# A planned order of instructions with fillers for TensorE, eight weight remainders moved to TensorE and ScalarE, and later due times for the second MoE

## The chip, the cores and the metric

The kernel runs on one core of one Trainium2 chip. The metric is the device time of one execution in microseconds (us). The engines are TensorE (PE in the profile; its weight loads are PEld), VectorE (DVE), ScalarE (ACT), GpSimd (POOL) and SyncE (SP), which issues all DMAs here. TensorE's clock has two levels, 1.2 and 2.4 GHz; the profile gives the granted share of the full one.

## The reference

```python
# x (4,8,768,32), a (4,8,768), B, C (4,8,768,16)
for each chunk:                       # linear attention with decay
    L = exp(cum_i - cum_j) * causal
    y = ((C B^T) * L) x + (C state) * exp(cum)
    state = exp(sum) * state + sum_j B_j x_j * exp(cum_end - cum_j)
x = y as (3072, 256)                  # tokens x model
xn = x / sqrt(mean(x*x) + 1e-6) * rms_g
x = (silu(xn @ w_gate) * (xn @ w_val)) @ w_out       # 256 -> 1536 -> 256
h = x @ w_in                                         # 256 -> 1024
solu = h * softmax(h)
out = layernorm(solu) * g_ln @ w_out2                # 1024 -> 256
```

## The kernel before

The 3072 tokens are 24 units of 128 tokens, and six blocks of four units. A unit passes through the attention (names `lpe`, `lx`, `ls`, `cb`, `mt`, `y`, `s2`, `sbd`), through the RMS norm (`sq`, `ms`, `ts`, `pw`, `rb`, `xc`, `xn`, `xh`, `xl`), a block of 512 tokens through the first MoE (per slice `f` of 128 of the 1536 columns: `gm` and `vm` of TensorE, `th`, `si`, `mu`, `ah`, `al` of ScalarE and VectorE, then `o0`, `o1`), and each unit again through the second MoE (`h`, `mx`, `ex`, `so`, `va`, `t`, `tc`, `tl`, `f`, `out`). Each product is three fp32r matmuls on operands that are split into a high part and a remainder (`xh`/`xl`, `wg_h`/`wg_l`).

The weights come in 26 pieces of 128 x 512 (0, 3, 6, ... gate, 1, 4, 7, ... value, 2, 5, 8, ... output of the first MoE, 18 to 21 and 22 to 25 the second MoE's). The host passes them as 64-bit words. For each piece VectorE makes the fp32 value in three instructions (`wc`, L116, L119, L122), ScalarE copies out the high part (`wh`, L129), and VectorE or GpSimd subtracts for the remainder (`w`, L133). An unused way (`w_lopair`, `w_locopy`, with `VIA_PE` empty) lets TensorE form the remainder in PSUM with the identity and the negative identity, and ScalarE copy it out. Pieces 0 to 17 are wanted during block 0.

The order is no hand-written list. Each operation is entered with an engine, an assumed duration, a due time and its dependences; `plan()` runs through time, takes for the engine that can begin first the ready operation that is due first, and the program is emitted in that order. Every engine then executes its own instructions strictly in the order of the plan, whatever the real durations are. Due times come from `PRO` (where block 0 is to begin), `FIRST` (length of block 0), `Y0`, `YPOS`, `YSPAN` (the attention units), `WGAP` (late weights), `HLAG` and `TAILGAP` (the second MoE's units). `MARGIN` makes the plan assume that a result comes later than it does. Buffers are rings (`BUFS`); an operation that needs a buffer still in use waits. PSUM tiles `y` and `po1` (odd units of block 0) hold one unit's attention output in columns 0 to 255, its state in 256 to 319, its sum of squares in 320 and the broadcast norm factor in 384 to 511.

```python
        if b + 1 < NB:
            lag = [HLAG[min(q, 1)] for q in (b, b + 1)]
            H = start[b + 1] + lag[0] + k * (start[b + 2] - start[b + 1] + lag[1] - lag[0]) / n
```

Of the kernel before, what the change touches and what calls it, by code (L numbers as in the profile page):

```python
# [11 lines left out]
AF = mybir.ActivationFunctionType  # L12
ALU = mybir.AluOpType
# [24 lines left out]
VALATE = 5.0
EARLY = (-1.0, 1.5, 4.0, 6.0)
NPE = 4  # L40
MARGIN = {"PE": 0.5}
CROW = 30.0
WGAP = 8.0
HLAG = (50.0, 26.0)
TRACE = None
BUFS = {"hc": 1, "t": 1, "y": 1, "pg": 1, "pv": 1, "po0": 1, "po1": 1, "L": 2, "bc": 2, "cd": 2, "xb": 2, "e1": 2,
        "u": AHEAD, "th": 3, "wt": 3, "uth": 1, "utl": 1, "xs": 3, "ah": 2, "al": 2, "sbd": 1, "sq": 1,
# [4 lines left out]
def fused_kernel(ctx, tc, aT, xbt, bcT, wg, wv, wo1, rg, wi2, wo2, gl, consts, out):  # L52
# [333 lines left out]
    def at_xc(u):  # L386
        d = st[u]
        d["xts"] = sp.tile([P, 2, P], F32, name="xts", bufs=BUFS["xts"])
        A.activation(d["xts"], d["y"][:, 0:256].rearrange("p (g i) -> p g i", g=2), AF.Copy)

    def at_xn(u):
        d = st[u]
        for g in range(2):
            V.scalar_tensor_tensor(out=d["xts"][:, g], in0=d["xts"][:, g], scalar=rgt[:, g:g + 1],
                                   in1=d["y"][:, 384:512], op0=ALU.mult, op1=ALU.mult)

    def at_xh(u):
        b, k = unit_blk[u]
# [290 lines left out]
    for u in range(NU):  # L689
# [59 lines left out]
        op(f"ts{u}", "DVE", 0.16, Y, (at_ts, u), after=[f"ms{u}"], use=[f"y{u}"])  # L749
        op(f"pw{u}", "POOL", 0.6, Y, (at_pw, u), after=[f"ts{u}"])  # L750
        op(f"rb{u}", "PE", 0.12, Y, (at_rb, u), after=[f"pw{u}"], use=[f"y{u}"])
        op(f"xc{u}", "ACT", 0.42, Y, (at_xc, u), after=[f"y{u}", f"sq{u}"], new=[("xts", f"xt{u}")], use=[f"y{u}", f"xt{u}"])
        op(f"xn{u}", "DVE", 0.6, Y, (at_xn, u), after=[f"rb{u}", f"xc{u}"], use=[f"y{u}", f"xt{u}"])
        op(f"xh{u}", "ACT", 0.42, Y, (at_xh, u), after=[f"xn{u}"] + ([f"xh{u-1}"] if k else []), new=[("xs", f"xs{b}")] if k == 0 else [],
           use=[f"xt{u}", f"xs{b}"])
        op(f"xl{u}", "DVE", 0.43, Y, (at_xl, u, V), after=[f"xh{u}"], use=[f"xt{u}", f"xs{b}"], lock=True)
# [46 lines left out]
    for u in range(NU):  # L803
        b, k = unit_blk[u]
        n = blk[b][1]
        if b + 1 < NB:
            lag = [HLAG[min(q, 1)] for q in (b, b + 1)]
            H = start[b + 1] + lag[0] + k * (start[b + 2] - start[b + 1] + lag[1] - lag[0]) / n
        else:
            H = start[NB] + 14 + TAILGAP * k  # L810
# [88 lines left out]

    op("sf", "PE", 0.7, 5.5, (c_suf,), new=[("t", "pd")], use=["pd"])  # L900
    op("wd", "ACT", 0.35, 5.5, (c_wdec,), after=["sf"], use=["pd"])
    op("cst", "SP", 0.9, 5, (ld_cst,), kb=128)
    op("glt", "SP", 0.45, 40, (ld_glt,), kb=4)
    for u in range(2):
        ops[f"sbd{u}"]["after"].append("cst")
        ops[f"xn{u}"]["after"].append("cst")

    early = [f"lpe{u}.{g}" for u in range(NPE) for g in range(2)] + ["e1p"] + ["cr0", "cr1"]
    ops["wh22"]["after"] += early + ["sf"]

    def plan():
        users = {}
# [44 lines left out]
                t = max(t, dma_end[-8])  # L957
            return t

        while len(order) < len(ops):  # L960
            best = None
            dve = None
            for e, names in ready.items():
                if e == "POOL":
                    names = names + [nm for nm in ready["DVE"] if "alt" in ops[nm] and nm != dve]
                c = [(est(ops[nm], e, MARGIN.get(e, 0.0) if free[e] > PRO else 0.0), nm) for nm in names]
                c = [x for x in c if x[0] < INF]
                if not c:
# [12 lines left out]
            if e != o["e"]:  # L981
                o = ops[nm] = dict(o, us=o["alt"][0], fn=o["alt"][1])
                ready["DVE"].remove(nm)
            else:
                ready[e].remove(nm)
            order.append((t, nm))
            if e == "SP":
                free[e] = t + o["us"]
                dma_free = max(dma_free, t + 1.3) + o["kb"] / 300.0
                end[nm] = dma_free + 1.0  # L990
                dma_end.append(end[nm])
            else:
# [18 lines left out]
    with tc.manual_schedule():  # L1011
        S.dma_start(la, aT)
        S.dma_start(um, consts[:, 0:3 * P])
        S.dma_start(ident, consts[:, 3 * P:4 * P])
        G.memset(ones, 1.0)
        G.memset(mhalf, -0.5)
        wu = pp.tile([P, 512], F32, name="wu", tag="y")
        for _ in range(WARM):
# [7 lines left out]
        V.tensor_scalar(out=cneg, in0=pc2[:, 0:192], scalar1=-1.0, scalar2=None, op0=ALU.mult)  # L1026
        V.tensor_copy(la16[0][:, 0:n16 * NS].rearrange("p (c n) -> p c n", n=NS),
                      la[:, 0:n16].unsqueeze(2).to_broadcast([P, n16, NS]))
        V.tensor_scalar(out=nid, in0=ident, scalar1=-1.0, scalar2=None, op0=ALU.mult)
        seq = plan()  # L1030
        if TRACE is not None:
            TRACE.append(seq)
        for _, nm in seq:
            fn, *a = ops[nm]["fn"]
            fn(*a)


# [62 lines left out]
```

## Time and profile before

| | us |
|---|---|
| median of three runs | 563.78 (561.93 to 565.23) |
| the profiled execution | 565.08 |
| its span, first to last instruction | 563.4 |
| TensorE busy | 546.5 |
| VectorE busy | 390.9 |
| ScalarE busy | 290.3 |
| GpSimd busy | 84.8 |
| mean granted clock of TensorE | 0.981 of full |

A matmul's end is modelled and reaches past the start of the next, so a busy TensorE isn't one at its peak; the distance from start to start tells its pace. The idle time that a row shows in front of an instruction is put down to the engine or DMA whose result came last.

### The profile page before, as it was taken

Reading aid. Unit: us, or ns where it says so; the run is one execution under the profiler, and the core shown is the slowest. Engines: PE = TensorE matmul, PEld = TensorE weight load, DVE = VectorE, ACT = ScalarE, POOL = GpSimd, SP = SyncE. Lnnn points to the kernel's source line nnn. Section 1 sums busy time; section 2 is a strip of 40 time slices with the busy share of each in tenths; the row PEclk is TensorE's granted clock in tenths of the full one; section 3 lists DMA queues with packets and bytes.
Section 4 is the critical chain, followed back from the end, with each engine's and each line's share of the span. In section 5 each row is a group of like instructions: output and inputs, shape, how many; then the busy total and the mean of one; then the engine's idle time right before and its main releaser. Section 6 shows DMA issues by size and latency. Waiting matters only on the chain.

```text
span 563.4 us, 9443 instructions
## 1 busy us (share of the span) xinstructions
PE 546.5 (97%) x3544; PEld 461.1 (82%) x3544; DVE 390.9 (69%) x789; ACT 290.3 (52%) x654; POOL 84.8 (15%) x118
## 2 busy tenths in 40 slices
PE   9879998899999999999999999999999999999996
PEld 8757886687888888888888888888888888888795
DVE  5788999999876776575684574684674574564763
ACT  6437654666555564463474454554543353343464
POOL 2333323212221010110111100110100000000010
PEclk9579999999999999999999999999999999999999
DMA  7464765542022021121120220220200000000000
GB/s 213 132 212 140 216 203 194 182 145 71 14 72 76 2 80 47 43 72 36 54 76 11 75 70 10 80 70 10 72 2 9 10 1 9 11 1 10 9 20 30
DMA packets 44366, 39.33 MB, mean 70 GB/s; under 512 B 3936, under 2 KB 36896, under 8 KB 44320
## 3 DMA queue, kind: packets, MB, share of 16 engines
q1 hardware_dynamic: 44320, 38.72, 22.5%
q8 instruction: 28, 0.46, 0.4%
q14 instruction: 18, 0.15, 0.1%
HBM read 35.37 MB, written 3.34 MB: 69 GB/s over the span
## 4 chain that ended last, share of the span: by engine, by line
PE 81%; DVE 15%; DMA 2%; issue 1%; ACT 1%; SPq 0%; POOL 0%; DVEq 0%; ACTq 0%; POOLq 0%
PE pv L558 15%; PE pg L558 15%; PE po L600 14%; PE ph L436 12%; PE pf L538 12%; PE pt L514 4%; PE pcb L301 3%; DVE wt L119 2%; PE y L326 2%; DVE wt L122 2%; DVE th L580 2%; PE y L321 1%; DVE al L592 1%; DVE th L576 1%; DVE L L307 1%; DVE wt L116 1%
## 5 line engine op out<-in xcount | busy, mean ns | idle before, releaser
L586 ACT ACTIVATE ah<-th 128x512 fp32r<-128x512 f32 x72 | 45.2, 628 | 52.2 <-PE po L600 38.8
L580 DVE TENSOR_TENSOR th<-pv,th 128x512 f32<-128x512 f32 x72 | 49.8, 691 | 29.2 <-PE pv L558 24.1
L592 DVE TENSOR_TENSOR al<-th,ah 128x512 fp32r<-128x512 f32 x70 | 49.3, 704 | 26.0 <-ACT ah L586 25.6
L576 DVE SCALAR_TENSOR_TENSOR th<-th,pg 128x512 f32<-128x512 f32 x72 | 49.1, 682 | 20.0 <-ACT th L572 19.7
L558 PE MATMUL pg<-xh,wg_h 128*128 128x512 f32 x144 | 59.5, 413 | 2.3 <-ACT xh L401 1.2
L600 PE MATMUL po<-ah,wo_h 128*128 128x512 f32 x144 | 60.3, 419 | 0.0
L600 PE MATMUL po<-al,wo_h 128*128 128x512 f32 x144 | 56.7, 394 | 2.3 <-DVE al L592 2.3
L558 PE MATMUL pv<-xh,wv_h 128*128 128x512 f32 x144 | 58.4, 406 | 0.0
L558 PE MATMUL pg<-xh,wg_l 128*128 128x512 f32 x144 | 57.0, 396 | 0.0
L558 PE MATMUL pg<-xl,wg_h 128*128 128x512 f32 x144 | 56.8, 394 | 0.0
L600 PE MATMUL po<-ah,wo_l 128*128 128x512 f32 x144 | 56.7, 394 | 0.0
L558 PE MATMUL pv<-xl,wv_h 128*128 128x512 f32 x144 | 56.5, 392 | 0.0
L558 PE MATMUL pv<-xh,wv_l 128*128 128x512 f32 x144 | 56.4, 392 | 0.0
L572 ACT ACTIVATE th<-pg 128x512 f32<-128x512 f32 x72 | 42.6, 592 | 26.6 <-PE pg L558 26.4
L502 POOL TENSOR_TENSOR sc<-sc,mhalf 128x1 f32<-128x1 f32 x24 | 14.1, 587 | 263.6 <-DVE sc L497 263.6
L237 ACT ACTIVATE L<-L,cneg 128x128 f32<-128x128 f32 x160 | 50.5, 390 | 0.6 <-DMA L<-crow 0.6
L460 ACT ACTIVATE ut<-ph,sc 128x1024 f32<-128x1024 f32 x20 | 22.3, 1116 | 54.5 <-DVE sc L447 54.5
L538 PE MATMUL pf<-wo_h,uth 128*128 128x256 f32 x176 | 49.6, 282 | 0.3 <-DVE utl L528 0.2
L538 PE MATMUL pf<-wo_h,utl 128*128 128x256 f32 x176 | 49.6, 282 | 0.0
L538 PE MATMUL pf<-wo_l,uth 128*128 128x256 f32 x176 | 49.5, 281 | 0.0
L447 DVE TENSOR_REDUCE sc<-ph 128x1 f32<-128x1024 f32 x20 | 24.5, 1225 | 31.7 <-PE ph L436 31.7
L523 ACT ACTIVATE uth<-pt 128x512 fp32r<-128x512 f32 x44 | 26.0, 595 | 31.1 <-PE pt L514 30.9
(138 smaller groups left out, 1225.2 us busy)
## 6 DMA issues: line engine op xcount, KB each, us to landing
L<-crow SPq DMA_DIRECT2D x20, 512.0 KB
stage<-in_wo_dram SPq DMA_DIRECT2D x10, 512.0 KB
xb<-in_xbt_dram SPq DMA_DIRECT2D x24, 192.0 KB
stage<-in_wg_dram SPq DMA_DIRECT2D x6, 512.0 KB
bc<-in_bcT_dram SPq DMA_DIRECT2D x48, 64.0 KB
stage<-in_wv_dram SPq DMA_DIRECT2D x6, 512.0 KB
out_dram<-ob SPq DMA_DIRECT2D x24, 128.0 KB
stage<-in_wi_dram SPq DMA_DIRECT2D x4, 512.0 KB
```

The costliest lines, as they stand in the source:

```text
L237: A.activation(d["L"][:, h], d["L"][:, h], AF.Exp, bias=cneg[:, u * 8 + h:u * 8 + h + 1])
L436: T.matmul(ph[c], xx[:, kk, k * P:(k + 1) * P], ww[:, kk, 512 * c:512 * c + 512], start=(i == 0), stop=(i == 5))
L447: V.tensor_reduce(out=sc[:, 0:1], in_=ph[0], axis=AX.X, op=ALU.max, negate=True)
L523: A.activation(d["uT"][0][:, 4 * c:4 * c + 4].rearrange("p k t -> p (k t)"), d["ptc", c], AF.Copy)
L538: T.matmul(d["pf"][:, 0:DM], uu[:, k], ww[:, k], start=(k == 0 and i == 0), stop=(k == 7 and i == 2))
L558: T.matmul(ps[:, :n], ww[:, kk, f * P:(f + 1) * P], xx[:, kk, :n], start=(i == 0), stop=(i == 5))
L572: A.activation(d["th"], d["pg"], AF.Tanh, scale=0.5)
L576: V.scalar_tensor_tensor(out=d["th"], in0=d["th"], scalar=1.0, in1=d["pg"], op0=ALU.add, op1=ALU.mult)
L580: V.tensor_tensor(out=d["th"], in0=d["pv"], in1=d["th"], op=ALU.mult)
L586: A.activation(d["ah"], d["th"], AF.Copy)
L592: e.tensor_tensor(out=d["al"], in0=d["th"], in1=d["ah"].bitcast(F32), op=ALU.subtract)
L600: T.matmul(po[b, m][:, :n], ww[:, f, m * P:(m + 1) * P], aa, start=(f == 0 and i == 0), stop=(f == NF - 1 and i == 2))
```

## The change

- `VIA_PE` names eight pieces (3, 4, 6, 7, 9, 10, 12, 13: gate and value pieces 1 to 4 of six), whose remainders TensorE and ScalarE form. The load of the identity, until now third in SP's queue, and its negation become operations of the plan.
- A filler `warm`: where the plan leaves TensorE idle for over 0.5 us before its time `PRO` + 6 and after the first `y`, some small matmuls of ones are put into the unused columns 322 to 383 of the last unit's `y` tile.
- `xc` of the norm multiplies with the gain `rms_g` on ScalarE (two instructions in place of one), and `xn` on VectorE is one multiplication in place of two.
- The plan's constants: `PRO` 34 to 31, `FIRST` 63 to 75, `YPOS`, `YSPAN`, `TAILGAP`, `SLACK0`; the weight operations get a margin of 0.5 us (`WMG`), and DMAs are planned at 280 in place of 300 bytes per ns (`DRATE`).
- `HLAG`: the second MoE's units of block 0 are due 70 (not 50) us behind the start of the next block, and the lag falls to 26 in steps up to block 4 (not at block 1).

```diff
-PRO = 34.0
-FIRST = 63.0
-VIA_PE = ()
+PRO = 31.0
+FIRST = 75.0
+VIA_PE = (3, 4, 6, 7, 9, 10, 12, 13)
-YPOS, YSPAN = 0.65, 1.0
-TAILGAP = 5.0
+YPOS, YSPAN = 0.55, 0.85
+TAILGAP = 3.0
-SLACK0 = 0.1
+SLACK0 = 0.3
-HLAG = (50.0, 26.0)
+HLAG = (70.0, 26.0, 4)
+WMG = 0.5
+DRATE = 280.0
+FILL = 0.7
...
-        A.activation(d["xts"], d["y"][:, 0:256].rearrange("p (g i) -> p g i", g=2), AF.Copy)
+        for g in range(2):
+            A.activation(d["xts"][:, g], d["y"][:, g * P:(g + 1) * P], AF.Copy, scale=rgt[:, g:g + 1])
...
-        for g in range(2):
-            V.scalar_tensor_tensor(out=d["xts"][:, g], in0=d["xts"][:, g], scalar=rgt[:, g:g + 1],
-                                   in1=d["y"][:, 384:512], op0=ALU.mult, op1=ALU.mult)
+        V.tensor_tensor(out=d["xts"], in0=d["xts"], in1=d["y"][:, 384:512].unsqueeze(1).to_broadcast([P, 2, P]), op=ALU.mult)
...
-            lag = [HLAG[min(q, 1)] for q in (b, b + 1)]
+            lag = [HLAG[0] + (HLAG[1] - HLAG[0]) * min(1.0, q / HLAG[2]) for q in (b, b + 1)]
...
+    op("idn", "SP", 0.45, 4, (ld_ident,), kb=64)
+    if VIA_PE:
+        op("nid", "DVE", 0.25, 6, (c_nid,), after=["idn"])
+        for i in VIA_PE:
+            ops[f"wp{i}"]["after"].append("nid")
...
+    def warm(u, n):
+        if u not in st:
+            return
+        for _ in range(n):
+            T.matmul(st[u]["y"][:, 322:384], ones, ones[:, 0:62], start=True, stop=True, skip_group_check=True)
...
+        def mg(nm, e):
+            if nm[0] == "w" and nm[1] != "d":
+                return WMG
+            return MARGIN.get(e, 0.0) if free[e] > PRO else 0.0
...
+            if nm[0] == "y":
+                lasty = int(nm[1:])
+            if e == "PE" and lasty is not None and t < PRO + 6 and t - free[e] > 0.5:
+                order.append((free[e], (warm, lasty, int((t - free[e]) * FILL / 0.22))))
             order.append((t, nm))
...
-                dma_free = max(dma_free, t + 1.3) + o["kb"] / 300.0
+                dma_free = max(dma_free, t + 1.3) + o["kb"] / DRATE
...
-        S.dma_start(ident, consts[:, 3 * P:4 * P])
...
-        V.tensor_scalar(out=nid, in0=ident, scalar1=-1.0, scalar2=None, op0=ALU.mult)
```

## Rows read from the trace of the kernel before

**Rows 1.** The page: busy us, share and instructions; granted clock in 40 slices.
```profile
PE 546.5 (97%) x3544; PEld 461.1 (82%) x3544; DVE 390.9 (69%) x789; ACT 290.3 (52%) x654; POOL 84.8 (15%) x118
...
PEclk9579999999999999999999999999999999999999
```

**Rows 2.** Windows: length, busy us (instructions) of PE, PEld, DVE, ACT, POOL, granted clock, DMA.
```profile
6.40:16.64 10.24, 8.29 (x100) 7.53 (x99) 8.39 (x16) 7.48 (x25) 3.55 (x5) 1.00 0.84 220
16.64:30.30 13.66, 13.66 (x101) 12.46 (x105) 8.61 (x21) 5.75 (x19) 6.01 (x8) 0.50 0.33 108
30.30:37.12 6.82, 5.34 (x70) 4.21 (x62) 5.84 (x17) 2.67 (x7) 2.41 (x4) 1.00 0.63 181
37.12:43.95 6.83, 4.21 (x10) 3.06 (x11) 6.41 (x15) 2.41 (x5) 1.27 (x2) 0.50 1.06 338
...
43.95:140.00 96.05, 91.66 (x606) 72.90 (x605) 93.02 (x172) 59.89 (x149) 27.73 (x31) 1.00 0.52 163
140.00:520.00 380.00, 380.00 (x2394) 321.82 (x2393) 242.86 (x480) 187.41 (x404) 40.63 (x60) 1.00 0.13 38
520.00:564.00 44.00, 38.03 (x253) 33.74 (x251) 24.73 (x68) 22.18 (x47) 2.75 (x5) 0.99 0.06 19
```

**Rows 3.** Chain that ended last, 0 to 60 us: start, us, what.
```profile
16.64 1.01 PE y L361 x4
...
40.22 2.96 PE pg L558 x6
```

**Rows 4.** Timeline at the first wait of TensorE in unit 0's norm.
```profile
15.96 0.38 ACT L389 ACTIVATE xts<-y 128x256 f32<-128x256 f32 x1
...
16.36 0.23 DVE L340 COPY s<-y 128x64 f32<-128x64 f32 x1 [0.64 <-ACT xts L389]
...
16.64 1.01 PE L361 MATMUL y<-ones,sq 128*128 128x1 f32 x4 [1.95 <-DVE s L340]
```

**Rows 5.** Timeline of TensorE at full clock: fp32 matmuls, an attention unit, fp32r matmuls.
```profile
32.31 1.08 PE L872 MATMUL pc<-um,la 128*96 128x256 f32 x4
...
33.23 0.61 PE L321 MATMUL y<-cd,sbd 128*128 128x128 f32 x4
...
129.99 0.61 PE L321 MATMUL y<-cd,sbd 128*128 128x128 f32 x4
...
132.30 0.50 PE L558 MATMUL pg<-xh,wg_h 128*128 128x512 f32 x1
132.63 0.39 PE L558 MATMUL pg<-xl,wg_h 128*128 128x512 f32 x1
132.87 0.40 PE L558 MATMUL pg<-xh,wg_l 128*128 128x512 f32 x1
```

**Rows 6.** Groups of TensorE between 60 and 140 us: two of nine.
```profile
L558 PE MATMUL pg<-xh,wg_h 128*128 128x512 f32 x30 | 12.4, 413 | 1.0 <-DVE th L576 1.0
...
L558 PE MATMUL pv<-xl,wv_h 128*128 128x512 f32 x28 | 10.9, 389 | 0.0
```

**Rows 7.** The remainder's line: duration ns min/median/max, first and last start.
```profile
L133 DVE TENSOR_TENSOR wv_l<-wt,wv_h x4: 681/684/690, 39.6 to 96.0; 128x512 fp32r<-128x512 f32 x4
L133 DVE TENSOR_TENSOR wg_l<-wt,wg_h x3: 680/683/684, 10.0 to 76.9; 128x512 fp32r<-128x512 f32 x3
...
L133 POOL TENSOR_TENSOR wg_l<-wt,wg_h x3: 1301/1321/1321, 32.5 to 91.0; 128x512 fp32r<-128x512 f32 x3
```

**Rows 8.** Groups by line of the whole span: busy us, mean ns, idle before.
```profile
L523 ACT ACTIVATE uth<-pt 128x512 fp32r<-128x512 f32 x44 | 26.0, 595 | 31.1 <-PE pt L514 30.9
...
L394 DVE SCALAR_TENSOR_TENSOR xts<-xts,rgt,y 128x128 f32<-128x128 f32 x48 | 14.4, 341 | 6.3 <-PE y L383 6.2
...
L405 DVE TENSOR_TENSOR xl<-xts,xh 128x256 fp32r<-128x256 f32 x24 | 10.4, 435 | 2.9 <-ACT xh L401 2.8
```

**Rows 9.** Timeline: one VectorE instruction, and what GpSimd ran then.
```profile
92.26 1.09 POOL L241 TENSOR_SCALAR_AFFINE_SELECT L<-L 128x1024 f32<-128x1024 f32 x1
...
92.35 1.55 DVE L119 SCALAR_TENSOR_TENSOR wt<-stage,wt 128x512 int32<-128x512 int32 x1
```

More of the change, by code (lines that the diff above doesn't have):

```diff
@@ L751, in fused_kernel @@
         op(f"rb{u}", "PE", 0.12, Y, (at_rb, u), after=[f"pw{u}"], use=[f"y{u}"])
-        op(f"xc{u}", "ACT", 0.42, Y, (at_xc, u), after=[f"y{u}", f"sq{u}"], new=[("xts", f"xt{u}")], use=[f"y{u}", f"xt{u}"])
-        op(f"xn{u}", "DVE", 0.6, Y, (at_xn, u), after=[f"rb{u}", f"xc{u}"], use=[f"y{u}", f"xt{u}"])
+        op(f"xc{u}", "ACT", 0.6, Y, (at_xc, u), after=[f"y{u}", f"sq{u}"], new=[("xts", f"xt{u}")], use=[f"y{u}", f"xt{u}"])
+        op(f"xn{u}", "DVE", 0.42, Y, (at_xn, u), after=[f"rb{u}", f"xc{u}"], use=[f"y{u}", f"xt{u}"])
         op(f"xh{u}", "ACT", 0.42, Y, (at_xh, u), after=[f"xn{u}"] + ([f"xh{u-1}"] if k else []), new=[("xs", f"xs{b}")] if k == 0 else [],
@@ L901, in fused_kernel, with ld_ident, c_nid @@
     op("wd", "ACT", 0.35, 5.5, (c_wdec,), after=["sf"], use=["pd"])
+    def ld_ident():
+        S.dma_start(ident, consts[:, 3 * P:4 * P])
+    def c_nid():
+        V.tensor_scalar(out=nid, in0=ident, scalar1=-1.0, scalar2=None, op0=ALU.mult)
+    op("idn", "SP", 0.45, 4, (ld_ident,), kb=64)
[3 more added lines that the diff above has]
+            ops[f"wp{i}"]["after"].append("nid")
+    ops["rb0"]["after"].append("idn")
     op("cst", "SP", 0.9, 5, (ld_cst,), kb=128)
@@ L905, in fused_kernel @@
         ops[f"sbd{u}"]["after"].append("cst")
-        ops[f"xn{u}"]["after"].append("cst")
+        ops[f"xc{u}"]["after"].append("cst")
     early = [f"lpe{u}.{g}" for u in range(NPE) for g in range(2)] + ["e1p"] + ["cr0", "cr1"]
     ops["wh22"]["after"] += early + ["sf"]
+    def warm(u, n):
[3 more added lines that the diff above has]
+            T.matmul(st[u]["y"][:, 322:384], ones, ones[:, 0:62], start=True, stop=True, skip_group_check=True)
     def plan():
@@ L958, in est @@
             return t
-        while len(order) < len(ops):
+        def mg(nm, e):
+            if nm[0] == "w" and nm[1] != "d":
+                return WMG
+            return MARGIN.get(e, 0.0) if free[e] > PRO else 0.0
+        lasty = None
+        while len(end) < len(ops):
             best = None
@@ L965, in plan @@
                     names = names + [nm for nm in ready["DVE"] if "alt" in ops[nm] and nm != dve]
-                c = [(est(ops[nm], e, MARGIN.get(e, 0.0) if free[e] > PRO else 0.0), nm) for nm in names]
+                c = [(est(ops[nm], e, mg(nm, e)), nm) for nm in names]
                 c = [x for x in c if x[0] < INF]
@@ L1033, in fused_kernel @@
         for _, nm in seq:
-            fn, *a = ops[nm]["fn"]
+            fn, *a = ops[nm]["fn"] if isinstance(nm, str) else nm
             fn(*a)
```

## Prediction

> **What bounds the kernel now.** I read the page first. TensorE is busy for 97% of the span and the next engine, VectorE, for 69%; the granted clock is below full in the second, third and fourth of forty slices alone [rows 1]. So what can be won must be idle time of TensorE or time at its lower clock, and work that is added to TensorE must fit into idle time.
>
> The windows show where such time is [rows 2]. From 140 to 520 us TensorE is busy in all 380.00 us: no due time can win anything there. From 43.95 to 140 us TensorE shows 91.66 of 96.05 us and VectorE 93.02, so here VectorE, which converts the weights beside its other work, is the fuller engine. Ahead of that is the prologue, the attention of the first four units, which ends with the first matmul of the first MoE at 40.22 us [rows 3]. In it the clock is granted at 0.50, that is 1.2 GHz, from 16.64 to 30.30 us, with TensorE busy in every one of these 13.66 us, and again from 37.12 to 43.95 us. The chain of waits runs through TensorE in the first of these stretches, from the first `ms` at 16.64 us on [rows 3]. Before the first fall TensorE was busy for 8.29 of 10.24 us; before the second for 5.34 of 6.82 [rows 2]. The tail after 520 us has 38.03 busy us of 44, and the last output must still leave the chip in it.
>
> What TensorE really has free in block 0 needs its pace. One fp32r matmul of 512 columns follows the other after 0.23 to 0.24 us [rows 5]. Nine groups of 28 to 30 such matmuls ran between 60 and 140 us, 260 in all [rows 6]: 260 x 0.23 = 59.8 us. Five attention units at 132.30 - 129.99 = 2.3 us each [rows 5] add 11.6, and I estimate 1 us for the small ones. That is 72.4 of 80 us: 7.6 us idle, or 9.1 when scaled to the 96 us of the stage.
>
> **The prologue: fillers, plan, clock.** If the first stretch ran at full clock, its 13.66 us of TensorE work would be 6.83. But VectorE has 8.61 us of work in it, so that at most 13.66 - 8.61 = 5.0 us are won there; from below, nothing. The fillers and the weight pieces that TensorE gets here both serve the clock, and ScalarE (5.75 us) has room for it. The weight margin and the lower DMA rate let the plan expect late weights, so that fewer instructions stand behind one that is late. I take 4.0 us, near the upper end, because TensorE's chain fills the whole stretch. From 40.22 to 43.95 us the first MoE runs at half clock; at full clock it saves 1.9. In front of it stands the chain of `rb`, `xn`, `xh` and `xl`, where the last unit's tile is already given up by the time that the filler would be emitted, so that no filler covers the wait for `xl`; only weight pieces can. I take half, 0.9. The identity's load leaves the head of SP's queue, and everything behind it is issued earlier by one issue, some 0.4 us; I take 0.3. Sum of the prologue: 4.0 + 0.9 + 0.3 = 5.2 us won, bounds 7.3 won and 4.4 lost (the second rival).
>
> What speaks against the fillers stands in the timeline: the first `ms` of unit 0 needs only `sq`, but waited until 16.64 us, for the copy of the state at 16.36, which reads other columns of the same PSUM tile [rows 4]. A filler writes into that tile too, so it stands behind every read of the tile that the plan put before it. It fills the wait for GpSimd's power, when no read is under way; in front of `ms` it would begin when `ms` could, and delay it. The Trainium skill (PSUM — Partial Sum Buffer, "PSUM bank collisions raise a hardware error") says the same as a rule: accesses of different engines have to be kept apart by the bank and not by the columns. By that rule the fillers ahead of `ms` win none of the 4.0 us; by the row alone, those ahead of `rb` still may.
>
> **Eight remainders.** A piece costs TensorE an fp32 matmul of 512 columns with the identity and an fp32r one. The trace has no fp32 matmul so wide; two of 256 columns take from 32.31 to 33.23 us, so 0.92 for 512 columns, and 0.92 + 0.23 = 1.15 us for a piece [rows 5]. Eight make 9.2. I count two in the prologue, where their time is part of the fillers' work, and six in block 0: 6.9 us. ScalarE gets eight copies out of PSUM of 0.595 us [rows 8], 4.8 us, hidden: it is busy for 59.89 of 96.05 us [rows 2]. If that cover were gone, the `tanh` behind a copy would come 0.6 us late.
>
> VectorE loses the remainders that it did itself: of the eight, by their starts in the timeline, four after 43.95 us (value pieces 3 and 4, gate pieces 2 and 4), at 0.684 each [rows 7], 2.7 us. Three of the others ran on GpSimd at 1.3 us. The norm's `xn` is now one instruction of 256 columns instead of two of 0.341; the nearest row, 256 columns at 0.435 [rows 8], makes 0.25 us less for each of the five or six units in block 0, 1.4 us. Its cost goes to ScalarE's second `xc`, which is hidden in the same way. GpSimd has less to do, so VectorE waits less for it: one of its instructions that takes about 0.69 elsewhere took 1.55 us while GpSimd's selection ran [rows 9]. The Trainium skill (SBUF — State Buffer, "SBUF: two separate sides") states that the two share a pair of ports under an exclusive lock; the row agrees with it, and by it the two removed GpSimd remainders in the stage would save VectorE up to two such stalls, 1.7 us. The selections stay, so I count 0.9 as one stall of the row. VectorE: 2.7 + 1.4 + 0.9 = 5.0 us less.
>
> So VectorE needs 5.0 us less in block 0, but TensorE needs 6.9 more of its 9.1 idle us. TensorE's floor in the stage becomes 96.05 - 9.1 + 6.9 = 93.9 us, a gain of 2.2 at best; from the other side, if none of its idle time can be used, 6.9 lost. Each of these matmuls also stands in TensorE's strict order behind `wc` of VectorE and `wh` of ScalarE, and everything behind it waits with it; that didn't exist before, since only `gm`, `vm` and `o` waited for weights. Both engines would be filled to some 95%, and each waits for the other in every slice. I take 0.
>
> **The rest.** The second MoE's later due times and the other constants change which work fills TensorE, in a stretch where it is full [rows 2]; they can win nothing there. Lost could be what a longer tail costs. For that I take as bounds a gain of 1 and a loss of 3 us, from half of the 44 - 38.03 = 6 us that the tail has idle; value 0.
>
> **The sum.** 565.1 (the profiled execution, 563.4 of span) - 5.2 + 0 + 0 = 559.9. The median of the runs is 1.3 lower than that execution, and so I forecast 558.6, rounded to **559 us**.
>
> **The rivals.**
>
> *The full gain.* The prologue wins 7.3 and block 0 2.2: 563.8 - 9.5 = 554.3. For it: VectorE has over a third of the first half-clock stretch free. Against: everything must fit. Chance 0.12.
>
> *The clock falls all the same: slower.* Place: the prologue, from the first `ms` on. The fillers wait for the tile's readers, begin late, and the clock is granted at 0.50 as before; now 0.7 of the idle 1.95 + 1.48 us before the two falls [rows 2] is filler, 2.4 us on TensorE's chain, and one weight piece at half clock, 2.3, stands in a stretch that was full already. With 0.3 won by the identity that is 4.4 lost: 563.8 + 4.4 = 568.2. It decides when the clock is still at half when the second unit's `y` runs. For it: the wait in [rows 4]. Against: fillers ahead of `rb` have no such reader. Chance 0.26.
>
> *TensorE becomes the bound of block 0.* The prologue wins its 5.2, but most of the 6.9 us of weight matmuls lie on TensorE's path, say 4.5: 563.8 - 5.2 + 4.5 = 563.1, no change that can be told. For it: the 9.1 idle us lie in many pieces. Against: VectorE gets 5.0 us free. Chance 0.20.
>
> *My forecast*, a gain of some 3 to 7 us: 0.42.
>
> About 0.5%, 2.8 us, is what a measurement of this kernel can tell from no change: 561.0 to 566.6. The forecast and the full gain make 0.54, of which I give 0.02 to no change: faster 0.52, same 0.22, slower 0.26. The range reaches from the full gain to the slow rival: 553 to 568; the likeliest case's own is 556 to 561.
>
> **What would show it.** In the new profile the first `gm` should begin at 34 to 36 us (40.22 before), with full clock between 17 and 30 us; fillers should appear ahead of `rb` with no idle time behind them. Between 44 and 140 us VectorE's busy share should fall below 95% and TensorE's visible idle time stay under 4 us; the line of the remainders should show fourteen subtractions on VectorE and GpSimd together in place of 22 and eight pairs of matmuls of 0.9 and 0.23 us. From 140 us to 510 TensorE should stay full. I am wrong if the clock falls at the same places, if the matmul of a weight piece shows waits of over 1 us on `wh`, or if the second MoE's late units leave TensorE idle after the last slice of block 5.

## The result, and the profile after

The changed kernel takes 570.89 us (median of four runs, 570.69 to 571.54), the kernel before 563.81 beside it (561.93 to 565.23). The ratio is 1.0135, 95% interval 1.0106 to 1.0164: slower by 7.6 us, where 559 was forecast. Below, a ratio r is also given as (r - 1) x 563.8 us.

The page of the changed kernel (its profiled execution took 570.95 us): span, busy time of TensorE and the others, granted clock in 40 slices.

```profile
span 569.2 us, 9519 instructions
...
PE 553.4 (97%) x3576; PEld 462.8 (81%) x3576; DVE 387.7 (68%) x761; ACT 302.3 (53%) x686; POOL 85.5 (15%) x114
...
PEclk9869999999999999999999999999999999999999
```

Against [rows 1] the span is 5.8 us longer and TensorE is busy 6.9 us longer; what TensorE has idle falls from 563.4 - 546.5 = 16.9 to 15.8 us. So the change gave TensorE more work and hardly filled a gap with it. The windows, in the columns of [rows 2], say where:

```profile
15.94:19.36 3.42, 3.42 (x17) 3.42 (x17) 1.97 (x5) 1.14 (x4) 1.51 (x3) 0.50 0.56 153
...
29.60:39.84 10.24, 8.70 (x48) 6.71 (x48) 8.16 (x18) 2.36 (x6) 2.50 (x4) 0.50 0.85 256
...
44.00:140.00 96.00, 93.05 (x599) 71.56 (x597) 89.40 (x160) 60.35 (x149) 20.47 (x23) 1.00 0.49 154
140.00:160.00 20.00, 19.04 (x116) 14.92 (x117) 17.11 (x28) 12.24 (x31) 7.21 (x7) 1.00 0.22 66
160.00:200.00 40.00, 39.49 (x253) 32.65 (x252) 28.45 (x54) 22.61 (x54) 7.39 (x10) 1.00 0.17 52
200.00:500.00 300.00, 300.00 (x1913) 255.07 (x1912) 182.41 (x359) 150.14 (x325) 34.19 (x46) 1.00 0.12 37
```

The first fall of the clock is shorter, 3.42 us in place of 13.66 [rows 2]; the second is longer, 10.24 in place of 6.83, and ends in the first MoE, as it did before. Together 13.7 us at 1.2 GHz against 20.5. In 43.95 to 140 us VectorE's busy share fell from 97% [rows 2] to 93%, and TensorE's rose from 95% to 97%. From 140 to 200 us, where TensorE was full [rows 2], it now idles for 1.5 us.

The chain around the start of the first MoE (start, us, what), after the answer to [rows 3]:

```profile
32.38 1.03 PE y L364 x4
33.44 0.17 DVE r L377
33.65 1.97 PE y L930 x8
35.62 0.23 PE y L386
35.87 0.43 DVE xts L397
36.38 0.42 ACT xh L403
36.85 2.96 PE pg L560 x6
39.81 1.46 PE pv L560 x6
```

The first `gm` starts at 36.85 us, 3.4 us earlier than in [rows 3] (how far one profile can tell this stands in the last section). The fillers (L930) stand in one place only, eight matmuls directly ahead of the last `rb`, and they are on the chain: 1.97 us at half clock, for which `rb`, `xn` and `xh` wait. In the timeline `rb` begins at 35.41 us, though GpSimd's power, which it needs, was done at 34.33. No weight piece is in the prologue: the first pair (L141, L142) stands behind the first twelve matmuls of the first MoE, and all eight lie in block 0. One costs what the distance from start to start shows in the timeline:

```profile
41.11 1.02 PE L141 MATMUL pw<-wt,ident 128*128 128x512 f32 x2
41.57 0.79 PE L142 MATMUL pw<-wg_h,nid 128*128 128x512 f32 x1
42.20 0.40 PE L560 MATMUL pg<-xh,wg_h 128*128 128x512 f32 x1
```

That is 42.20 - 41.11 = 1.09 us, eight make 8.7. The account of TensorE's busy time closes: 8.7 for the pairs + 2.0 for the fillers - 3.4 (half of the 6.8 us that no longer run at half clock) = 7.3, measured 6.9. Seven of the eight pairs start behind 44 us, 7.6 us: without them TensorE did 93.05 - 7.6 = 85.4 us of block 0's own work up to 140 us, where the kernel before did 91.66 [rows 2]. The work of block 0 came later, although it began earlier: the first output matmul of block 1, the 73rd of L602, starts at 124.37 us, before (L600) at 120.06.

The second MoE begins at 161.89 in place of 142.59 us (its first `h` in the timeline, of the kernel after, then of the one before):

```profile
161.89 0.40 PE L438 MATMUL ph<-wi_h,xh 128*128 128x512 f32 x1
```

```profile
142.59 0.40 PE L436 MATMUL ph<-wi_h,xh 128*128 128x512 f32 x1
```

and in its first units the chain leaves TensorE, for VectorE and ScalarE, for almost 10 us. (TensorE has other work meanwhile; from 160 to 200 us it is idle for 0.51 us.)

```profile
184.89 2.78 PE ph L438 x12
...
187.70 1.24 DVE sc L449
...
188.96 1.21 ACT ut L462 x2
...
196.67 0.69 DVE utl L530
...
197.40 0.65 PE pt L516 x4
```

### The profile page after: what moved, and what is told of

It is laid out like the page before. It is cut to its first block, busy times and chain, and to the rows that moved or that the text cites. A ratio compares the mean times of both kernels' runs of the same rounds, so it can differ in the third digit from the quotient of the medians.

```text
span 569.2 us, 9519 instructions
## 1 busy us (share of the span) xinstructions
PE 553.4 (97%) x3576; PEld 462.8 (81%) x3576; DVE 387.7 (68%) x761; ACT 302.3 (53%) x686; POOL 85.5 (15%) x114
## 4 chain that ended last, share of the span: by engine, by line
PE 79%; DVE 14%; ACT 3%; issue 2%; DMA 2%; SPq 0%; DVEq 0%; ACTq 0%
PE po L602 15%; PE pg L560 14%; PE pv L560 14%; PE ph L438 12%; PE pf L540 12%; PE pt L516 4%; PE pcb L304 3%; DVE th L582 2%; DVE wt L122 2%; PE y L329 2%; DVE th L578 2%; DVE al L594 1%; DVE wt L125 1%; PE y L324 1%; DMA xb<-in_xbt_dram 1%
## 5 line engine op out<-in xcount | busy, mean ns | idle before, releaser
L602 PE MATMUL po<-ah,wo_h 128*128 128x512 f32 x144 | 60.0, 417 | 0.0
L594 DVE TENSOR_TENSOR al<-th,ah 128x512 fp32r<-128x512 f32 x65 | 45.8, 705 | 19.8 <-ACT ah L588 18.9
L602 PE MATMUL po<-ah,wo_l 128*128 128x512 f32 x144 | 56.7, 394 | 0.0
L602 PE MATMUL po<-al,wo_h 128*128 128x512 f32 x144 | 56.5, 392 | 0.0
L449 DVE TENSOR_REDUCE sc<-ph 128x1 f32<-128x1024 f32 x20 | 24.5, 1224 | 35.5 <-PE ph L438 35.5
L560 PEld LDWEIGHTS pg<-xh,wg_h 128*128 128x128 f32 x144 | 27.3, 189 | 14.2 <-DVE th L578 6.0
```

Source lines behind the costliest of these rows:

```text
L449: V.tensor_reduce(out=sc[:, 0:1], in_=ph[0], axis=AX.X, op=ALU.max, negate=True)
L560: T.matmul(ps[:, :n], ww[:, kk, f * P:(f + 1) * P], xx[:, kk, :n], start=(i == 0), stop=(i == 5))
L594: e.tensor_tensor(out=d["al"], in0=d["th"], in1=d["ah"].bitcast(F32), op=ALU.subtract)
L602: T.matmul(po[b, m][:, :n], ww[:, f, m * P:(m + 1) * P], aa, start=(f == 0 and i == 0), stop=(f == NF - 1 and i == 2))
```

## The experiments

Eighteen kernels were timed. A name that begins with b_ is the kernel before with an edit, one with a_ the changed kernel with an edit. A table at the end sets most of them side by side.

**The eight pairs.** In a_novia the changed kernel has no pairs and the plan is made anew; b_via is the kernel before with the pairs alone; a_small and a_dbl keep the order of the changed kernel and cut each pair to 8 columns (38.68 - 38.43 = 0.25 us in its timeline, so 8 x 0.84 = 6.7 us less) or issue it twice (8.7 us more); a_nomm leaves the pairs' matmuls out.

```diff
@@ a_novia @@
-VIA_PE = (3, 4, 6, 7, 9, 10, 12, 13)
+VIA_PE = ()
@@ b_via @@
-VIA_PE = ()
+VIA_PE = (3, 4, 6, 7, 9, 10, 12, 13)
@@ a_small @@
-        T.matmul(pv, ident, w_f32(i), start=True, stop=False)
-        T.matmul(pv, nid, pieces[i][2][0], start=False, stop=True)
+        T.matmul(ps[:, 0:8], ident, wtm[i].bitcast(F32)[:, 0:8], start=True, stop=False)
+        T.matmul(ps[:, 0:8], nid, pieces[i][2][0][:, 0, 0:8], start=False, stop=True)
...
-        A.activation(pieces[i][2][1], wtm[i, "ps"].rearrange("p (k f) -> p k f", k=2), AF.Copy)
+        ps = wtm[i, "ps"]
+        A.activation(pieces[i][2][1], ps[:, 0:1].unsqueeze(2).to_broadcast([P, 2, 256]), AF.Copy)
@@ a_dbl @@
-        T.matmul(pv, ident, w_f32(i), start=True, stop=False)
-        T.matmul(pv, nid, pieces[i][2][0], start=False, stop=True)
+        for _ in range(2):
+            T.matmul(pv, ident, w_f32(i), start=True, stop=False)
+            T.matmul(pv, nid, pieces[i][2][0], start=False, stop=True)
@@ a_nomm @@
-        A.activation(pieces[i][2][1], wtm[i, "ps"].rearrange("p (k f) -> p k f", k=2), AF.Copy)
+        A.activation(pieces[i][2][1], w_f32(i), AF.Copy)
...
-            fn(*a)
+            if fn is not w_lopair:
+                fn(*a)
```

a_novia: 

> The changed kernel with no piece by way of TensorE, planned anew: the remainders return to VectorE and GpSimd. Theory A: 8.7 us of TensorE work go, up to 5 us of VectorE work return, of which at most 2.7 show: 562 to 565 us, with the first gm still at about 37 us. Theory B (order and due times make the loss): 569 us or more.

Measured 569.17 us, ratio 1.0103 (1.0034 to 1.0172): without any pair the kernel is still 5.8 us slower than before (1.9 to 9.7), as theory B had it. So the pairs aren't the whole loss; what share they have, this wide interval can't say.

b_via: 

> The kernel before with the eight pieces by way of TensorE and ScalarE as its only change, planned anew. Theory A: 563.8 + 8.7 - up to 2.7 = 570 to 572.5 us. Theory B: 562 to 566 us, since the matmuls fit into the 9 us that TensorE has idle in block 0.

Measured 566.81 us, ratio 1.0072 (1.0041 to 1.0103), 4.1 us slower. By the pages TensorE is busy 552.4 us, 5.9 more than before, in a span of 566.0, which leaves 13.6 idle, 3.3 less than before. The time lies between the two theories' ranges: the pairs' 8.7 us are paid for in part. How much of that is VectorE's relief isn't shown, since b_via also has another order, which alone can cost some us (see below).

a_small: 

> The changed kernel in its own order, the eight matmul pairs cut to 8 of 512 columns (the remainders are then wrong); everything that waits for them and the buffers' holding times stay. Some 7.7 us of TensorE time go. Theory A (price in full): 563 us. Theory C (part of the pairs lies in time in which TensorE would wait for VectorE anyway; the run with the pieces as the only change kept 5.2 of 8.1 us so): 566.5 to 568.5 us. Theory B (the order alone): 570 us or more.

Measured 567.26 us, ratio 1.0078 (1.0052 to 1.0104), 3.2 us less than the changed kernel and in theory C's range.

a_dbl: 

> The changed kernel in its own order, each of the eight matmul pairs issued twice: 8.7 us more TensorE work in the same places. Theory A: 579.5 us. Theory C: the idle time is used up by the first pair, so that the second costs more than the first, 576 to 580 us. Theory B: under 574 us.

Measured 576.26 us, ratio 1.0243 (1.0195 to 1.0291), 6.1 us more, also as theory C had it. One us of pairs costs 3.2 / 6.7 = 0.5 to 6.1 / 8.7 = 0.7 us of time, in the same order of instructions; the intervals leave room for far less and for the full price.

a_nomm: 

> The changed kernel in its own order, with the eight identity matmul pairs of the weight remainders left out: ScalarE copies the fp32 piece itself, so the remainders are wrong and only the time counts. Theory A (TensorE has no idle time that these matmuls can use, each pair of about 1.09 us lies on its path in full): 570.9 - 8.7 = 562 us. Theory B (the matmuls fit into idle time, and the loss comes from the new order and the due times): 568 us or more.

Measured 575.86 us, ratio 1.0211 (1.0169 to 1.0253), slower than with the matmuls. This run decides nothing: the fp32 piece now stays in its buffer until ScalarE has copied it, and VectorE's next conversion waits for that copy (2.9 and 2.4 us in the waits of L119), a wait that the changed kernel doesn't have.

**Fillers and due times.**

```diff
@@ a_nofill @@
-FILL = 0.7
+FILL = 0.0
@@ a_hlag @@
-HLAG = (70.0, 26.0, 4)
+HLAG = (50.0, 26.0, 1)
```

a_nofill: 

> The changed kernel in its own order without the fillers. The trace after has fillers in one place alone, eight records of 1.97 us at half clock directly ahead of the last rb of the prologue. Theory A (they lie on the chain to the first gm and don't move the clock): the first gm 1.0 to 1.8 us earlier and 569.1 to 569.9 us. Theory B (they keep or bring back the clock): the half-clock stretch gets longer and the time is 571 us or more.

Measured 568.89 us, ratio 1.0091 (1.0059 to 1.0122), 2.5 us less than with fillers, about theory A's gain. Its timeline has the wait that they filled:

```profile
34.66 0.32 PE L386 MATMUL y<-ident,r 128*128 128x128 f32 x1 [0.99 <-POOL r L382]
36.01 0.52 PE L560 MATMUL pg<-xh,wg_h 128*128 128x512 f32 x1 [1.02 <-ACT xh L403]
```

It is 0.99 us long, and the eight fillers took 1.97 at half clock.

a_hlag: 

> The changed kernel with the second MoE's lags of before (50, 26, from block 1 on), planned anew. Theory D (the later due times cost the 3 us that TensorE loses between 140 and 200 us): 567 to 568.5 us. Its rival (weights and attention lose them there whatever the lag): 570 us or more.

Measured 568.32 us, ratio 1.0104 (1.0073 to 1.0136), 1.7 us less, in theory D's range; TensorE is busy for 59.65 of the 60 us from 140 to 200, in place of 58.53. Both intervals overlap with that of the changed kernel, so each is a sign and not a size.

**The plan's constants, without pairs, fillers, norm or due times.** b_pro is the kernel before with the moved identity, PRO, SLACK0, WMG and DRATE.

```diff
-PRO = 34.0
+PRO = 31.0
-SLACK0 = 0.1
+SLACK0 = 0.3
+WMG = 0.5
+DRATE = 280.0
...
+    op("idn", "SP", 0.45, 4, (ld_ident,), kb=64)
+    ops["rb0"]["after"].append("idn")
...
```

b_pro: 

> The kernel before with only what changes the plan's start: the identity's load in the plan, the margin for weight operations, 280 for DMAs, PRO 31, SLACK0 0.3; no piece by TensorE, no filler, the old norm and due times. Theory E (an earlier first gm is worth nothing, since VectorE converts the weights until about 135 us and sets the end of block 0): first gm at 35 to 38 us and 562 to 566 us. Theory F (my prediction's step: what the prologue wins stays won): 558 to 560 us.

Measured 569.61 us, ratio 1.0112 (1.0063 to 1.0161). Both theories missed: the prologue is won, and the kernel is 6.3 us slower. The chain of its trace, just behind the start of block 0, shows where what was won is lost:

```profile
39.45 0.70 DVE th L582
...
41.53 0.61 DVE wt L121
...
42.17 0.69 DVE wt L124
42.86 0.35 DVE wt L118
...
43.23 1.65 DVE wt L121
...
44.90 1.64 DVE wt L124
46.54 0.61 DVE th L578
...
47.19 1.63 PE pg L560 x6
```

```profile
34.59 0.80 PE L560 MATMUL pg<-xh,wg_h 128*128 128x512 f32 x1 [1.21 <-ACT xh L403]
...
47.19 0.50 PE L560 MATMUL pg<-xh,wg_h 128*128 128x512 f32 x1 [3.66 <-DVE th L578]
```

The first `gm` starts at 34.59 us, 5.6 earlier than in [rows 3], and the first output matmul (L602) at 41.97 in place of 47.53; the twelfth, at 60.74, is 1.1 us later than before. Between them the third slice's `gm` waits until 47.19 for `th`, in front of which five instructions of weight conversion stand in VectorE's order. Two of these take 1.64 us in place of 0.69, while GpSimd ran a selection (43.22 to 44.32) and a remainder of a weight (44.43 to 45.99). The Trainium skill (SBUF — State Buffer, "SBUF: two separate sides") has the two engines share ports under a lock, with which these rows agree, as [rows 9] did. From 44 to 60 us TensorE then is busy for 12.81 of 16, and the clock falls again:

```profile
44.00:60.00 16.00, 12.81 (x86) 10.40 (x87) 13.08 (x19) 6.65 (x17) 4.66 (x5) 0.79 0.23 77
```

This gave theory G: the constants push the conversions of the early pieces back in VectorE's strict order, and block 0 starts early only to wait for them. The planned order has it: the last conversion of piece 3 stands 36th among VectorE's operations before, 51st in b_pro, 54th after. Three runs take the constants one by one:

```diff
@@ b_wmg @@
+WMG = 0.5
...
+        def mg(nm, e):
+            if nm[0] == "w" and nm[1] != "d":
+                return WMG
+            return MARGIN.get(e, 0.0) if free[e] > PRO else 0.0
@@ b_sl @@
-SLACK0 = 0.1
+SLACK0 = 0.3
@@ a_early @@
-SLACK0 = 0.3
+SLACK0 = 0.1
-DRATE = 280.0
+DRATE = 300.0
...
-            if nm[0] == "w" and nm[1] != "d":
-                return WMG
```

b_wmg: 

> The kernel before with one edit: the weight operations are planned with a margin of 0.5 us. Theory G (the plan's margins push the conversion of the weights back in VectorE's strict order, and block 0 then waits for them): in VectorE's order the last conversion of piece 3 stands 15 instructions further back than before, of piece 2 nine; so first gm no later than before (40 us), end of block 0 (the first copies of the last unit's output) later by 4 to 10 us, and 567 to 570 us. Rival H (the margin by itself does nothing; the loss of the constants together comes from the DMA rate or from their combination): 562 to 565.5 us.

Measured 569.15 us, ratio 1.0099 (1.0080 to 1.0118), in theory G's range.

b_sl: 

> The kernel before with one edit: SLACK0 0.1 to 0.3, by which the plan's choice before block 0 may take an operation that could begin 0.3 us later, if it is due earlier. Nothing of it names a weight, but in VectorE's order the last conversion of piece 3 stands 14 instructions further back. Theory G: as with the margin, 566 to 570 us. Rival H: 562 to 565.5 us. A second rival, that only the margin counts since it also holds in block 0: 562 to 565.5 here and 567 to 570 with the margin alone.

Measured 569.46 us, ratio 1.0104 (1.0074 to 1.0133). Either constant alone costs nearly what all cost together, 5.6 and 5.9 us against 6.3; rival H falls, and so does the second rival.

a_early: 

> The changed kernel with three constants of the plan put back (no weight margin, SLACK0 0.1, 300 bytes per ns), so that the weights are converted earlier: in VectorE's order the last conversion of piece 2 stands at 24 in place of 34, of piece 3 at 46 in place of 54. The eight pairs, the fillers and the later second MoE stay. Theory G: 565 to 568 us, some 4 us of what the constants cost. Rival (the loss lies in the pairs, the fillers and the second MoE alone): 569.5 to 572 us.

Measured 566.92 us, ratio 1.0060 (1.0045 to 1.0075): with the three constants put back, 4.2 us of the loss of 7.6 are gone, as theory G forecast. (All four executions had a granted clock of 0.990 to 0.994; the kernel before took 561.1 to 562.8 us at 0.990 to 0.993, so at an equal clock a_early is 4 to 6 us slower, and some of the 4.2 us can be the clock.) Its windows and chain also say what full clock in the prologue is worth:

```profile
14.73:21.55 6.82, 6.00 (x36) 5.74 (x40) 3.79 (x9) 3.57 (x12) 2.52 (x4) 0.50 0.40 114
21.55:44.00 22.45, 18.89 (x177) 13.98 (x170) 19.31 (x43) 10.95 (x30) 5.19 (x8) 1.00 0.76 236
```

```profile
35.32 0.60 DVE wt L125
35.92 0.07 DVE r L377
35.99 0.34 DVE wt L119
36.36 0.70 DVE wt L122
37.09 0.70 DVE wt L125
37.81 0.64 ACT wo_h L132
...
39.17 0.34 DVE xl L407
```

```profile
38.80 0.50 PE L560 MATMUL pg<-xh,wg_h 128*128 128x512 f32 x1 [0.44 <-ACT xh L403]
```

The clock is at half for 6.8 us only, in place of 20.5. Still the first `gm` starts at 38.80, just 1.4 us before that of [rows 3]: once TensorE is fast, the chain runs through VectorE's conversions, while TensorE idles for 22.45 - 18.89 = 3.6 us.

**The norm's edit.** b_xn is the kernel before with the norm's new instructions and their new assumed durations; b_xn_order has the same instructions with the old assumed durations, so that the order of the program stays as it was, operation by operation.

```diff
@@ b_xn, b_xn_order @@
-        A.activation(d["xts"], d["y"][:, 0:256].rearrange("p (g i) -> p g i", g=2), AF.Copy)
+        for g in range(2):
+            A.activation(d["xts"][:, g], d["y"][:, g * P:(g + 1) * P], AF.Copy, scale=rgt[:, g:g + 1])
...
-        for g in range(2):
-            V.scalar_tensor_tensor(out=d["xts"][:, g], in0=d["xts"][:, g], scalar=rgt[:, g:g + 1],
-                                   in1=d["y"][:, 384:512], op0=ALU.mult, op1=ALU.mult)
+        V.tensor_tensor(out=d["xts"], in0=d["xts"], in1=d["y"][:, 384:512].unsqueeze(1).to_broadcast([P, 2, P]), op=ALU.mult)
@@ b_xn alone: the assumed us @@
-        op(f"xc{u}", "ACT", 0.42, Y, (at_xc, u),
-        op(f"xn{u}", "DVE", 0.6, Y, (at_xn, u),
+        op(f"xc{u}", "ACT", 0.6, Y, (at_xc, u),
+        op(f"xn{u}", "DVE", 0.42, Y, (at_xn, u),
```

b_xn: 

> The kernel before with the norm's edit alone: the gain multiplied by ScalarE in two instructions, one multiplication by VectorE in place of two. By the prediction's price, 0.25 us of VectorE for each unit of block 0, 562 to 564 us. Theory G: the planned order shifts too (piece 3 stands 11 instructions further back in VectorE's order), so that the same edit costs: 565 to 568 us.

Measured 575.33 us, ratio 1.0205 (1.0178 to 1.0232): 11.6 us slower, more than any theory had. Most of it lies in one place, in its windows and in its timeline: TensorE runs short, the clock falls for 10.24 us, and in the midst of it a norm's `ms` waits 3.32 us for `xc`, which waits for the state's update (L342) that VectorE reaches only behind its conversions. These are of the second MoE's pieces (`wi`), not of the early ones that theory G speaks of: the 66th output matmul of the first MoE still starts at 104.77 us, before at 105.32, and the 96th at 149.00, before at 136.98.

```profile
102.00:112.48 10.48, 6.87 (x62) 5.01 (x60) 10.34 (x17) 6.13 (x16) 2.18 (x2) 1.00 0.45 141
112.48:122.72 10.24, 6.30 (x16) 4.87 (x17) 8.51 (x18) 4.00 (x11) 1.00 (x2) 0.50 0.60 208
```

```profile
114.20 1.01 PE L361 MATMUL y<-ones,sq 128*128 128x1 f32 x4 [3.32 <-ACT xts L390]
```

b_xn_order: 

> The norm's edit as before, but the plan keeps its old assumed durations, so that the order of the program is that of the kernel before, operation by operation. If the edit's loss of 11.6 us came with the shifted order: 562 to 564.5 us, which is also what the prediction's price of 1.4 us less on VectorE gives. If the second instruction of ScalarE costs by itself: 566 us or more.

Measured 563.57 us, ratio 1.0002 (0.9981 to 1.0023). The instructions in the old order cost nothing and win nothing that can be told; the 11.6 us are the order to which two new assumed durations led the plan. The prediction's price for them was right, as the groups by line of this run show beside [rows 8]: one instruction of 412 ns in place of two of 341.

```profile
L390 ACT ACTIVATE xts<-y,rgt 128x128 f32<-128x128 f32 x48 | 15.0, 367 | 8.5 <-DVE s L342 6.2 <-DVE s L340 2.3
...
L394 DVE TENSOR_TENSOR xts<-xts,y 128x256 f32<-128x256 f32 x24 | 9.9, 412 | 4.2 <-PE y L383 4.1
```

**Is it the weights, or any other order?** If small edits move the time so much, a rival of G must be tried (K): the order before is a chosen one, and any other is worse. b_m6 and b_y6 shuffle over 400 planned operations and leave pieces 0 to 8 at most a place or so from where they were; b_w3late moves piece 3 alone; b_wdue makes the first MoE's weights due earlier; a_back takes the constants, the fillers and the due times out of the changed kernel at once.

```diff
@@ b_m6 @@
-MARGIN = {"PE": 0.5}
+MARGIN = {"PE": 0.6}
@@ b_y6 @@
-YPOS, YSPAN = 0.65, 1.0
+YPOS, YSPAN = 0.6, 1.0
@@ b_w3late @@
+    ops["wc3.0"]["after"].append("mt3.1")
@@ b_wdue @@
-            return gdue(0, 2 * c + (LAG if q == 2 else 0)) - 4.0
+            return gdue(0, 2 * c + (LAG if q == 2 else 0)) - 8.0
@@ a_back: as a_early, and @@
-HLAG = (70.0, 26.0, 4)
-FILL = 0.7
+HLAG = (50.0, 26.0, 1)
+FILL = 0.0
```

b_m6: 

> The kernel before with TensorE's margin in the plan at 0.6 in place of 0.5 us, an edit with no meaning of its own: 419 of the planned operations change places, but the conversions of pieces 0 to 9 stand where they stood in VectorE's order (2, 12, 21, 36, 55, ...). Theory G (what costs is the conversion of early pieces further back): 562 to 565.5 us. Rival K (the order before is a chosen one, and nearly any other that the plan gives is worse, wherever the weights stand): 566.5 to 570 us.

Measured 566.02 us, ratio 1.0047 (1.0022 to 1.0071), between the two theories' ranges.

b_y6: 

> A second order without a meaning of its own: the kernel before with YPOS 0.60 in place of 0.65 (when the attention of the later units is due). 428 planned operations change places, the conversions of pieces 0 to 8 stand where they stood or one place later. Theory K, by the 2.0 us that the first such order cost: 565.5 to 569 us. Theory G: 562 to 565 us.

Measured 566.93 us, ratio 1.0069 (1.0046 to 1.0092), in K's range: with the early pieces where they were, this order costs 3.9 us, so the place of the early pieces isn't the only cause.

b_w3late: 

> The kernel before with one dependence added: VectorE begins piece 3 (the second gate piece) only behind the last mask of unit 3. Its last conversion stands at 51 in place of 36 in VectorE's order, where the margin alone and SLACK0 alone put it; pieces 0 to 2 and 4 to 6 stand as before. Theory G: 567 to 570 us. Rival K, which takes any other order for worse, gives the same; so this run counts only with the one whose weights stay. If it is 562 to 565.5 us, the place of piece 3 is not the cause and G falls.

Measured 567.60 us, ratio 1.0052 (1.0021 to 1.0083), no more than the two orders without a meaning. So the place of piece 3 alone isn't told apart from a mere change of order.

b_wdue: 

> The kernel before with the first MoE's weights due 4 us earlier in the plan: 360 planned operations change places, pieces 0 to 8 stand as before, pieces 9 and 10 two and four places further forward, piece 12 four further back, and the plan's own last time is 544.8 in place of 546.7 us. If weights that come earlier win time: 560 to 563.5 us. Theory K (nearly any other order is worse): 565 to 569 us. If neither: 563.5 to 565 us.

Measured 562.88 us, ratio 0.9987 (0.9960 to 1.0015). The median lies in the range for a gain, but the interval holds no change, so a gain isn't shown. It is another order that costs nothing, so K in its strict form falls as well.

a_back: 

> The changed kernel with the three constants of the plan put back as in the last but one run, without fillers, and with the old due times of the second MoE; pairs, norm and the other constants stay. If the shares measured so far add up (566.9, less 2.0 for the fillers, less 2.6 for the due times): 561 to 564 us. If they overlap: 565 to 567 us.

Measured 567.50 us, ratio 1.0077 (1.0050 to 1.0104), no better than a_early. The shares (which the expectation took from medians, 2.0 and 2.6 us, in place of 2.5 and 1.7 by ratios) don't add up.

| kernel | ratio | us against before | span | TensorE busy | idle |
|---|---|---|---|---|---|
| before | 1 | 0 | 563.4 | 546.5 | 16.9 |
| after | 1.0135 | +7.6 | 569.2 | 553.4 | 15.8 |
| b_via (pairs) | 1.0072 | +4.1 | 566.0 | 552.4 | 13.6 |
| b_pro (constants) | 1.0112 | +6.3 | 567.7 | 546.8 | 20.9 |
| b_wmg | 1.0099 | +5.6 | 567.6 | 544.6 | 23.0 |
| b_sl | 1.0104 | +5.9 | 567.0 | 545.0 | 22.0 |
| b_xn | 1.0205 | +11.6 | 574.2 | 549.7 | 24.5 |
| b_xn_order | 1.0002 | +0.1 | 562.5 | 544.8 | 17.7 |
| b_m6 / b_y6 | 1.0047 / 1.0069 | +2.6 / +3.9 | 561.9 / 567.7 | 542.4 / 549.2 | 19.5 / 18.5 |
| b_wdue | 0.9987 | -0.7 | 562.7 | 547.4 | 15.3 |
| a_novia | 1.0103 | +5.8 | 567.8 | 547.4 | 20.4 |
| a_early / a_back | 1.0060 / 1.0077 | +3.4 / +4.3 | 565.2 / 565.5 | 550.4 / 551.1 | 14.8 / 14.4 |

Spans and busy times are those of the profiled execution, from the page; idle is their difference. One profile of a kernel isn't all of it: b_xn_order has the order of the kernel before, and 1.7 us less of TensorE's busy time and 0.8 us more idle. So differences of 1 or 2 us in these columns say nothing. The table reads in two halves. What has no pairs leaves TensorE's work nearly alone, and idle time is added to it, 4 to 8 us where the constants or the norm's durations are changed. What has pairs has less idle time, but more work than it saves. The changed kernel has both, and I read its nearly unchanged 15.8 us as their sum: the pairs take up part of the waits that the constants make. No version is faster than the kernel before by more than its interval.

## Why the prediction was wrong

**The prologue: 3.4 us in this profile in place of 5.2, by other means, and not passed on.** The step that failed is "Sum of the prologue: 4.0 + 0.9 + 0.3 = 5.2 us won", taken whole into the time of the kernel. The first `gm` came at 36.85, just behind the forecast of 34 to 36. But b_pro won 5.6 us there and was 6.3 us slower: all that it had won was gone by the twelfth output matmul. What held TensorE up there was VectorE, still busy with conversions; time in the prologue is also time in which VectorE converts. a_early had the whole later prologue at full clock for 1.4 us. The prediction had the row for it, VectorE with 93.02 of 96.05 us [rows 2], and used it for block 0 alone. That VectorE sets the pace in every version is argued from this row, not shown. Nor is a better clock worth nothing: in an unchanged order it goes with a shorter time (last section).

The means failed too. "The fillers and the weight pieces that TensorE gets here both serve the clock": the pieces were not there, and the fillers, from 33.65 us on, stand behind the first fall. b_pro has neither, and its first fall is as short (14.56 to 17.98 us):

```profile
14.56:17.98 3.42, 3.42 (x19) 3.42 (x18) 2.06 (x6) 1.41 (x6) 1.67 (x3) 0.50 0.69 208
```

And the 4.0 us were priced from the 13.66 us that one profile had at half clock; b_xn_order, in the same order, has 6.83 us in its first fall (17.28 to 24.11). That the size came near (a mean of 5.1 us over several profiles, last section) is in part luck. What did shorten the prologue isn't shown; b_pro, with the constants and the moved identity alone, has its first `gm` at 34.59 us.

**The constants: a cost was left out.** That the margin and the rate "let the plan expect late weights, so that fewer instructions stand behind one that is late" was told as a gain without a price. The margin alone and SLACK0 alone cost 5.6 and 5.9 us in the kernel before; the two and DRATE together cost 4.2 in the changed one. For b_pro the trace shows the mechanism (five instructions of conversion in front of `th`). How much of it is the weights' place and how much any new order costs stays open: orders without a meaning cost 2.6 and 3.9 us, that of b_wdue nothing, and piece 3 alone 2.9 (1.2 to 4.7).

**The fillers.** Feared ahead of `ms`, they stood ahead of the last `rb`, on the chain, at half clock, and took longer than the wait that they fill. Without them it was 2.5 us less, a sign and not a size. The prediction had them in every unit's wait for GpSimd's power; the plan saw idle time in one.

**The second half of the clock's gain (0.9) did not come:** the first MoE ran at half clock from 36.85 to 39.84 us. No piece stood ahead of it, where the prediction had counted two.

**The pairs: priced right, paid for wrongly.** 1.09 us were measured for 1.15 forecast; eight, not six, are in block 0, 8.7 us for 6.9. The remainders by subtraction are fourteen as forecast. The step "I take 0" failed: by the ratios, 0.5 to 0.7 of each us of pairs remain in the time; b_via, with pairs and another order, is 4.1 us (2.3 to 5.8) slower. That is the third rival's mechanism with its price of 4.5, without the rival's other half, a prologue that stays won.

**The norm:** 0.27 us less of VectorE for each unit, 0.25 forecast, and in the old order no time.

**The rest:** the due times, "value 0", cost 1.7 us by overlapping intervals, inside the bounds, but the place was wrong: not the tail (49.2 - 43.78 = 5.4 us idle behind 520 us, and the same before, since that span ends at 563.4 and not at the 564 of the window), but 140 to 200 us, where a full window was taken for proof that nothing could be lost.

Four signs came as forecast: the first `gm` within a microsecond of its range, VectorE's share below 95%, TensorE's visible idle time at 96.00 - 93.05 = 2.95 us, fourteen subtractions. Two didn't: full clock between 17 and 30 us (it came at 19.36, and fell again at 29.60), and a full TensorE from 140 us on. The time went the other way all the same, since a busy share says how full an engine is and not how much of its work is new. The slower rival, a clock that falls all the same, had 568.2; its time was near (570.89 were measured), its cause wasn't: the first fall was 10 us shorter.

## What to carry to other kernels

Where a planner writes the order, each change of an assumed duration, a margin or a due time is also another program: first find out what an edit without a meaning costs (here 2.6 and 3.9 us), and test a new instruction in the old order. Set side by side executions with the same granted clock. A start that comes earlier counts only if the engine that feeds the next stage has its work done as well; look at what that engine does in the time that was won. A busy engine with idle time in many small pieces isn't free: ask what share of each added microsecond will remain (here 0.5 to 0.7, with wide intervals).

## What was not expected of the hardware

The changed kernel, a_small, a_dbl, a_nomm and a_hlag have the same instructions in the same order up to the first `gm`, but their profiles have it at 36.85, 34.15, 33.24, 33.51 and 33.39 us. The clock's changes lie at other times from the start of the program: a_small has one fall, from 26.96 to 37.20 us, a_dbl two, to 18.08 and from 31.73 us on, and the changed kernel two others (its windows above). The order of before spreads as much: 40.22 us in its own profile, 40.34 and 40.26 in b_y6 and b_wdue, 38.60 in b_xn_order, 37.02 in b_m6. So a difference of 3 us in the prologue of one profile isn't exact, those of b_pro and a_early included; their medians are what counts. Five profiles of each order don't overlap, though, so the prologue did get shorter: their means are 39.3 and 34.2 us, 5.1 apart.

```profile
34.15 0.80 PE L561 MATMUL pg<-xh,wg_h 128*128 128x512 f32 x1 [1.02 <-ACT xh L404]
```

```profile
33.24 0.79 PE L561 MATMUL pg<-xh,wg_h 128*128 128x512 f32 x1 [1.02 <-ACT xh L404]
```

```profile
38.60 0.79 PE L557 MATMUL pg<-xh,wg_h 128*128 128x512 f32 x1 [1.17 <-ACT xh L400]
```

```profile
37.02 0.80 PE L558 MATMUL pg<-xh,wg_h 128*128 128x512 f32 x1 [1.21 <-ACT xh L401]
```

(The timelines of a_small, a_dbl, b_xn_order and b_m6.) The whole time goes with the clock as well. Of the 74 executions of the kernel before beside the experiments, the 15 with a mean granted clock of 0.981 took 564.8 to 566.2 us, the 7 with 0.993 took 561.1 to 561.9: some 4 us, without any edit. Where the stretches at half clock lay in them isn't recorded.

The clock can also fall in block 0: in b_xn at 112.48 us, behind a stretch in which TensorE had been busy for 6.87 of 10.48 us, and back at 122.72. There a late instruction of VectorE costs twice, by the wait and by the pace of the matmuls behind it.
